# Seven copies on VectorE, one held score and a single PSUM tile in a fused attention and token-mixing kernel

## The chip, the cores and the metric

The kernel runs on one core of one Trainium2 chip. The metric is the device time of one launch in microseconds; for the kernel before it is 1265.29 us, the median of three runs (1265.22 to 1266.12).

## The reference

One input x of 2048 tokens by 512 channels goes through two branches, which a gate per token mixes:

```python
x = A_x
g = _sigmoid((x * gate_w).sum(-1, keepdims=True))
a = _A_ref(x, A_wqkv, A_wo)                   # softmax attention, H = 32 heads of Dh = 16
b = _B_ref(x, B_w1, B_b1, B_w2, B_b2)         # LayerNorm, then an MLP over the token axis (2048 -> 1792 -> 2048)
return g * a + (1 - g) * b
```

In the attention, `scores = q k^T * Dh**-0.5`, `p = softmax(scores)`, `o = p v`, and `o` is multiplied by `wo`. All of it is float32. The scores are the bulk of the elementwise work: 32 heads of 2048 by 2048, each of which has to go through an exponential.

## The kernel before

The first 278 us or so transpose x, project q, k and v, and run the first layer of the MLP. From there to about 1230 us runs the attention, with the second layer of the MLP, late query projections and output projections laid beside it. A short end (about 33 us) finishes the output.

**Groups, phases, scores.** The attention goes over 32 groups (`NG`), each two heads by half of the queries. A group has four phases (`PHASES`), so there are 128 in all. Each phase computes 16 score tiles of 128 keys by 512 queries (`NSC`), one matmul each (line 1067). A score matmul uses only one half of the rows of TensorE's array; the other half takes one "dense" matmul of the MLP or of a projection (line 1076), which runs at the same time. Most phases have 14 dense matmuls, some 12, and the last ones none.

**What happens to a score.** It lands in one of 7 PSUM banks (`BANKS`); the eighth holds the dense sum (`dn`). It takes one of three ways out. A single (`SINGLE`, six of the sixteen) is read by ScalarE, which writes exp of it to SBUF (line 1093). A pair (`TWO`, two pairs in adjacent banks) is read by one ScalarE instruction over 1024 columns (line 1031). A copied score (`EVAC`, six) is copied by VectorE from PSUM to one SBUF tile `pe` (line 1089), and at the end of the phase a single ScalarE instruction over 3072 columns takes the exponential in place (line 1102).

**Second product.** After the 16 scores TensorE multiplies exponentials by v (`apply_v`, line 963), two scores at a time, into a bank that VectorE then adds to the group's sum `ot` in SBUF (line 985). A phase applies its own singles and pairs (`TURNS`, five pairs of scores) and the copied scores of the phase before (`HELD`, three pairs of scores), since those get their exponential last. At the first phase of a group the held ones still belong to the group before, and go to a bank of their own.

**Order.** The attention is written under a manual schedule: instructions of each engine run in the order of the code, and a dependency tracker puts a semaphore wait before an instruction that touches a tile which another engine is still using. The banks are given out by hand: `shares` names which banks go to the pairs, the copies and the second product, and every score gets a PSUM tile of its own (`s0` to `s6`, then `t` for a pair, `u` for a copied score, `av`) from a pool that is opened twice in a phase (`regions`).

**Weights.** `load_weight` (line 133) brings raw blocks of the MLP's weights into `w_raw`, with four buffers; `split_weight` splits each in two parts. The first layer, before the attention, takes 64 blocks, the second layer 64 more.

Of the kernel before, what the change touches and what calls it, by code (L numbers as in the profile page):

```python
# [9 lines left out]
F32 = mybir.dt.float32  # L10
# [3 lines left out]
AF = mybir.ActivationFunctionType  # L14
# [6 lines left out]
PSUM = bass.MemoryType.PSUM  # L21
# [39 lines left out]
def gated_mix(ctx: ExitStack, tc: tile.TileContext, a_x, a_wqkv, a_wo, b_w1, b_b1, b_w2, b_b2, gate_w, out):  # L61
# [35 lines left out]
    mv = const.tile([P, NS, 2], F32, name="mv")  # L97
    rs = const.tile([P, NS], F32, name="rs")

    const.tile([P, 16], F32, name="pad")  # L100
# [34 lines left out]
    def load_weight():  # L135
        if blocks:
            src = blocks.pop(0)
            raw = wk.tile([P, NB], F32, name="w_raw", bufs=4)
            if len(src.shape) == 2:
                raw = raw[:, : src.shape[1]]  # L140
                dst = raw
            else:
                raw = raw[:, : src.shape[1] * P]
                dst = raw.rearrange("p (k s) -> p k s", s=P)
            with tc.issue_after(x_load.ins):
                nc.sync.dma_start(dst, src)
            loaded.append(raw)
# [768 lines left out]
    token, mark = (out_pool.tile([1, 1], F32, name=name, bufs=1) for name in ("token", "mark"))  # L916
# [7 lines left out]
    def shares(n):  # L924

        for one in range(0, BANKS, 2):
            lows = [k for k in range(one)][::2] + [k for k in range(one + 1, BANKS)][::2]
            for third in lows:
                if n in (third, third + 1):
                    first, second = (low for low in lows if low != third)  # L930
                    return [first, first + 1, one, second, second + 1, 2 * third + 1 - n, n]


    def regions():
        return tc.tile_pool(name="ps_s", bufs=1, space=PSUM, reuse_waits="tile")

    sums, latest, evac_done = {}, {}, []

# [49 lines left out]

    engines = {getattr(mybir.EngineType, name) for name in ("PE", "Activation", "DVE", "Pool", "SP")}
    with tc.manual_schedule(engines=engines):  # L990
        held, fence, turn, spare = [], None, 0, 0
        landed.clear()

        for p in range(LAST + 1):
# [14 lines left out]
            n_b = len(beside)  # L1009
            half = slice(0, HALF) if second else slice(HALF, P)  # L1010

            head = [second if n < n_b else (second + NSC - 1 - n) % 2 for n in range(NSC)]
            if n_b == NSC - 2:
                head[-2:] = second, 1 - second
            else:
                head[-4:] = second, 1 - second, 1 - second, second
            in_turn = list(range(n_b)) + ([14, 15] if n_b == NSC - 2 else [12, 13, 15, 14])
            qbs = {}
            for a, b in TURNS + HELD:
                if head[a] == head[b]:  # L1020
# [3 lines left out]
                    qbs[zero], qbs[one] = turn, 1 - turn  # L1024
                    turn = 1 - turn

            def exps(n):
                pt = ptp.tile([P, 2, NB], F32, name="p2", bufs=len(TWO))
                where = [share[(j - BANKS) % BANKS] for j in (n - 1, n)]
                low = min(where)  # L1030
                pairs_done.append(nc.scalar.activation(pt, twos[low, low + 1], AF.Exp, scale=SCALE))  # L1031
                for j, k in zip((n - 1, n), where):
                    units[j] = *units[j][:3], pt[:, k - low, :]

            pairs_done = []
            evac = evp.tile([P, len(EVAC), NB], F32, name="pe")
            units = {}
            share = shares(spare)
            pool = regions()
            psum = pool.__enter__()  # L1040
            ones = [psum.tile([P, NB], F32, name=f"s{n}") for n in range(BANKS)]
            for n in in_turn:
                i, qb = head[n], qbs[n]
                c = at[i][qb]
                at[i][qb] += 1
                if n < TWO[0][0]:
                    if n >= BANKS:
                        ones[share[n - BANKS]] = psum.tile([P, NB], F32, name=f"s{share[n - BANKS]}")
                    s = ones[share[n % BANKS]]
                else:  # L1050
                    if n == TWO[0][0]:
                        pool.__exit__(None, None, None)
                        pool = regions()
                        psum = pool.__enter__()
                        twos = {}
                        for low in range(BANKS):
                            if low == share[2]:
                                av = psum.tile([P, NB], F32, name="av")
                            elif low in (share[0], share[1]):
                                twos[low] = psum.tile([P, NB], F32, name=f"u{low}")  # L1060
                            elif low not in twos:
                                two = psum.tile([P, 2, NB], F32, name=f"t{low}")
                                twos[low], twos[low + 1] = two[:, 0, :], two[:, 1, :]
                                twos[low, low + 1] = two
                    s = twos[share[(n - BANKS) % BANKS]]
                rows_i = slice(i * HALF, i * HALF + ROWS)
                nc.tensor.matmul(  # L1067
                    s,
# [5 lines left out]
                if n < n_b:  # L1074
# [7 lines left out]
                if n == in_turn[-2]:  # L1082
                    if n_b and second and beside[-1][-1] in between:
                        between[beside[-1][-1]]()
                    for what, *args in amid.get(p, ()):
                        what(*args)
                if n in EVAC:
                    pt = evac[:, EVAC.index(n), :]
                    nc.vector.tensor_copy(pt, s)  # L1089
                    units[n] = i, c, qb, pt  # L1090
                elif n in SINGLE:
                    pt = ptp.tile([P, NB], F32, name="p1", bufs=len(SINGLE))
                    one = nc.scalar.activation(pt, s, AF.Exp, scale=SCALE)  # L1093
                    if n == SINGLE[-1] and p:
                        tc.add_manual_dep(one.ins, earlier.ins.name, SYNC, reason=EARLY)
                    units[n] = i, c, qb, pt
                else:
                    units[n] = i, c, qb, None
                    if n in (TWO[0][1], TWO[1][1]):
                        exps(n)  # L1100
            for x in ([evac] if p < LAST else [evac[:, :2, :], evac[:, 2:, :]]):
                done = nc.scalar.activation(x, x, AF.Exp, scale=SCALE)  # L1102
            tc.add_manual_dep(done.ins, pairs_done[0].ins.name, SYNC, reason=EARLY)
            evac_done.append(done)
            earlier = pairs_done[1]
            if n_b and second and beside[-1][-1]:
                beside[-1][-1]()
            if p == 0:
# [13 lines left out]
            spare = share[2]  # L1122
            if ph == 0:
                if held:
                    apply_v(av, grp - 1, held, final=True)
                    spare = share[3]
# [15 lines left out]
            pool.__exit__(None, None, None)  # L1142
            held = now_held
            if ph == PHASES - 1:
                assert at == [[NS, NS], [NS, NS]]


    with (
# [162 lines left out]
```

## Time and profile before

| what | value |
|---|---|
| median of three runs | 1265.29 us |
| the profiled execution's own span | 1263.6 us |
| TensorE, VectorE, ScalarE busy, of the span | 1255.3, 851.3, 1069.0 us (99, 67, 85%) |
| granted TensorE clock, mean of the span | 0.998 |
| first score of the attention | at 277.8 us |
| ScalarE busy between 400 and 1100 us | 100 us of each 100 |
| a phase in the middle of the attention (701.63 to 709.05 us) | 7.42 us |

The engines are PE (TensorE matmul), PEld (its weight load), DVE (VectorE), ACT (ScalarE), POOL and SP. Matmuls are pipelined, so PE reads as busy from the start of one to the modelled end of the next; a busy share of 99% does not say that it runs at its peak. A row of the timeline gives start, time taken, engine, line, operation and tiles, and in brackets how long the engine sat idle before it and what ended that. A row of the windows gives, after the stretch, the busy time of PE, PEld, DVE, ACT and POOL, then the granted clock, the share of the DMA engines and GB/s.

### The profile page before, as it was taken

Reading aid. Unit: us, or ns where it says so; the run is one execution under the profiler, and the core shown is the slowest. Engines: PE = TensorE matmul, PEld = TensorE weight load, DVE = VectorE, ACT = ScalarE, POOL = GpSimd, SP = SyncE. Lnnn points to the kernel's source line nnn. Section 1 sums busy time; section 2 is a strip of 40 time slices with the busy share of each in tenths; the row PEclk is TensorE's granted clock in tenths of the full one; section 3 lists DMA queues with packets and bytes.
Section 4 is the critical chain, followed back from the end, with each engine's and each line's share of the span. In section 5 each row is a group of like instructions: output and inputs, shape, how many; then the busy total and the mean of one; then the engine's idle time right before and its main releaser. Section 6 shows DMA issues by size and latency. Waiting matters only on the chain.

```text
span 1263.6 us, 32707 instructions
## 1 busy us (share of the span) xinstructions
PE 1255.3 (99%) x13342; PEld 828.5 (66%) x13342; DVE 851.3 (67%) x1562; ACT 1069.0 (85%) x1405; POOL 198.9 (16%) x316
## 2 busy tenths in 40 slices
PE   9999999999999999999999999999999999999997
PEld 7888888875666666666666666666666666666666
DVE  5675453178767676767677677776777677678883
ACT  4443343269999999999999999999999999999990
POOL 0220444461010101010101101111111111000000
PEclk9999999999999999999999999999999999999999
DMA  4799443243744444544344443443543442366611
GB/s 132 252 333 334 145 120 105 83 129 108 214 122 104 89 102 85 157 86 97 77 105 93 97 93 84 91 88 79 114 102 71 91 100 60 56 164 177 152 59 70
DMA packets 100555, 152.31 MB, mean 121 GB/s; under 512 B 17109, under 2 KB 56171, under 8 KB 96300
## 3 DMA queue, kind: packets, MB, share of 16 engines
q1 hardware_dynamic: 99820, 149.08, 45.9%
q8 instruction: 107, 1.75, 0.6%
q10 hardware_dynamic: 576, 1.05, 0.2%
q14 instruction: 52, 0.43, 0.1%
HBM read 105.39 MB, written 44.68 MB: 119 GB/s over the span
## 4 chain that ended last, share of the span: by engine, by line
PE 99%; ACT 1%; DVE 0%; issue 0%
PE av L963 31%; PE s L1067 22%; PE acc L424 12%; PE t L1067 9%; PE acc L75 8%; PE t L963 5%; PE dn L1076 4%; PE u L1067 3%; PE pa L1162 2%; PE acc L199 1%; PE acc L268 1%; PE acc L245 0%; ACT p L1093 0%; ACT pe L1102 0%; PE dn L1162 0%; PE pa L1192 0%
## 5 line engine op out<-in xcount | busy, mean ns | idle before, releaser
L1093 ACT ACTIVATE p<-s 128x512 f32<-128x512 f32 x768 | 412.4, 791 | 0.1
L1102 ACT ACTIVATE pe<-pe 128x3072 f32<-128x3072 f32 x129 | 381.7, 2961 | 0.0
L1067 PE MATMUL s<-qs,ks 64*128 64x512 f32 x1280 | 330.2, 400 | 0.6 <-ACT p L1093 0.6
L1089 DVE COPY pe<-s 128x512 f32<-128x512 f32 x512 | 318.2, 683 | 4.8 <-PE s L1067 1.1
L1067 PEld LDWEIGHTS s<-qs,ks 64*128 64x128 f32 x1280 | 225.6, 184 | 93.3 <-issue 45.3
L1031 ACT ACTIVATE p<-t 128x1024 f32<-128x1024 f32 x256 | 278.5, 1265 | 0.0
L963 PE MATMUL av<-p,v 128*32 128x256 f32 x3880 | 227.1, 379 | 0.0
L1089 DVE COPY pe<-u 128x512 f32<-128x512 f32 x256 | 164.9, 686 | 72.0 <-PE u L1067 72.0
L963 PE MATMUL av<-pe,v 128*32 128x256 f32 x3072 | 192.5, 383 | 0.0
L985 DVE TENSOR_TENSOR ot<-av,ot 128x512 f32<-128x512 f32 (+2 forms) x160 | 93.2, 583 | 142.3 <-PE av L963 141.0
L68 POOL TENSOR_TENSOR w_lo<-w_raw,w_hi 128x512 fp32r<-128x512 f32 (+1 forms) x128 | 153.1, 1203 | 197.3 <-ACT w_hi L67 100.3
L1076 PE MATMUL dn<-u_hi,w_hi 64*128 64x512 f32 x448 | 181.1, 404 | 0.0
L963 PEld LDWEIGHTS av<-p,v 128*32 128x32 f32 x3880 | 126.0, 110 | 83.3 <-ACT p L1093 0.2
L1076 PE MATMUL dn<-u_hi,w_lo 64*128 64x512 f32 x448 | 180.6, 403 | 0.0
L1076 PE MATMUL dn<-u_lo,w_hi 64*128 64x512 f32 x448 | 180.4, 403 | 0.0
L1067 PE MATMUL t<-qs,ks 64*128 64x512 f32 x512 | 142.2, 412 | 0.0
L963 PEld LDWEIGHTS av<-pe,v 128*32 128x32 f32 x3072 | 86.7, 109 | 82.1 <-ACT p L1093 37.8
L1080 POOL MEMSET token<- 1x1 f32 x128 | 11.4, 89 | 742.2 <-PE dn L1076 701.7
L67 ACT CAST w_hi<-w_raw 128x512 fp32r<-128x512 f32 (+1 forms) x67 | 38.0, 569 | 82.9 <-PE acc L424 63.1
L1067 PEld LDWEIGHTS t<-qs,ks 64*128 64x128 f32 x512 | 72.9, 184 | 51.0 <-ACT p L1093 49.5
L424 PE MATMUL acc<-h_hi,w_hi 128*128 128x512 f32 x224 | 87.9, 392 | 0.0
L424 PE MATMUL acc<-h_hi,w_lo 128*128 128x512 f32 x224 | 87.8, 392 | 0.0
(171 smaller groups left out, 1616.0 us busy)
## 6 DMA issues: line engine op xcount, KB each, us to landing
w_raw<-in_B_w_dram SPq DMA_DIRECT2D x96, 256.0 KB
ks<-kp SPq DMA_DIRECT2D x192, 128.0 KB
qs<-qp SPq DMA_DIRECT2D x256, 64.0 KB
kp<-pc SPq DMA_DIRECT2D x16, 512.0 KB
qp<-pc SPq DMA_DIRECT2D x8, 768.0 KB
qp<-row SPq DMA_DIRECT2D x24, 256.0 KB
v<-v SPq DMA_DIRECT2D x4, 1088.0 KB
x<-in_A_x_dram SPq DMA_DIRECT2D x16, 256.0 KB
```

The costliest lines, as they stand in the source:

```text
L67: copy(hi, src)
L68: return sub(lo, src, hi.bitcast(F32), ALU.subtract)
L75: nc.tensor.matmul(ps, a, b, start=start and n == 0, stop=stop and n == last)
L424: nc.tensor.matmul(p, a, b, start=first and k == 0, stop=last and k == 2)
L963: mm = nc.tensor.matmul(av[32 * j : 32 * (j + 1), i * QC : (i + 1) * QC], vb[b][:, v_at : v_at + 32], pt[:, h * QC : (h + 1) * QC], start= ...
L985: latest["add"] = nc.vector.tensor_tensor(x, y, x, ALU.add)
L1031: pairs_done.append(nc.scalar.activation(pt, twos[low, low + 1], AF.Exp, scale=SCALE))
L1067: nc.tensor.matmul(s, kt[grp][rows_i, c * P : (c + 1) * P], qt[grp][rows_i, qb * NB : (qb + 1) * NB], start=True, stop=True,)
L1076: mm = nc.tensor.matmul(ps, a[half], b[half], start=begin and not second, stop=last and bool(second))
L1089: nc.vector.tensor_copy(pt, s)
L1093: one = nc.scalar.activation(pt, s, AF.Exp, scale=SCALE)
L1102: done = nc.scalar.activation(x, x, AF.Exp, scale=SCALE)
```

## The change

The 16 scores of a phase get their way out from a string, `KINDS = "esesaaeseseeesbb"`: `e` is copied by VectorE, `s` is a single of ScalarE, `aa` and `bb` are the two pairs. So seven scores are copied, five are singles. The in-place exponential covers 3584 columns instead of 3072. The nine scores that ScalarE reads straight from PSUM are an odd number, so the last single (score 13) is held over with the seven copies: four pairs of scores are held, four are applied in their own phase. The pool of singles keeps six buffers.

The banks come from `given_out`, a small planner that walks through the 128 phases with fixed costs while the program is built, and notes for each score the bank that it takes to be free first. All seven banks are now one PSUM tile, `banks` (128 x 7 x 512), allocated once; scores, pairs and second products are slices of it. `shares`, `regions` and the per-score PSUM tiles are gone.

To make room in SBUF for the larger `pe`, `w_raw` has three buffers instead of four, `inv` one instead of two, and `token` and `mark` take the place of a pad.

```diff
-            raw = wk.tile([P, NB], F32, name="w_raw", bufs=4)
+            raw = wk.tile([P, NB], F32, name="w_raw", bufs=3)
...
-        t = out_pool.tile([P, w], F32, name="inv")[: n * DH]
+        t = out_pool.tile([P, w], F32, name="inv", bufs=1)[: n * DH]
...
-    EVAC = 1, 3, 5, 8, 14, 15
-    SINGLE = 0, 2, 4, 6, 7, 9
-    TWO = (10, 11), (12, 13)
-    TURNS = [(0, 2), (4, 6), (7, 9), *TWO]
-    HELD = [(1, 3), (5, 8), (14, 15)]
+    KINDS = "esesaaeseseeesbb"
+    SINGLES = 6
+    EVAC = [n for n, kind in enumerate(KINDS) if kind == "e"]
+    SINGLE = [n for n, kind in enumerate(KINDS) if kind == "s"]
...
+    own = sorted([(n, n) for n in SINGLE] + [(two[1], n) for two in TWO for n in two])
+    own = [n for _, n in own]
+    kept = list(EVAC)
+    if len(own) % 2:
+        own.remove(SINGLE[-1])
+        kept.append(SINGLE[-1])
+    TURNS, HELD = ([(x[i], x[i + 1]) for i in range(0, len(x), 2)] for x in (own, kept))
+    def given_out():
+
+        free, vector, scalar, stream, load, wide = [0.0] * BANKS, 0.0, 0.0, 0.0, 0.0, 0.0
+        given = []
+
+        def first_free(spread=1, at=None):
+            ways = [b for b in range(BANKS + 1 - spread)] if at is None else [at]
+            best = min(ways, key=lambda b: (max(free[b : b + spread]), b))
+            when = max(free[best : best + spread])
+            free[best : best + spread] = [1e9] * spread
+            return best, when
+
+        for p in range(LAST + 1):
...
+            for n, kind in enumerate(KINDS):
+                alone = n < singles or (n - singles) % 2 == 0
+                if kind in "es":
+                    bank[n], when = first_free()
...
+                scored[n] = start + 0.44
+                if kind == "e":
+                    vector = max(vector + 0.6, scored[n] + 0.69)
+                    free[bank[n]] = vector
+                    copied.append(vector)
+                elif kind == "s":
+                    scalar = max(scalar + 0.488, scored[n] + 0.6)
+                    free[bank[n]] = readers[n] = scalar
...
+            given.append(([bank[n] for n in range(NSC)], [b for b, _ in sums]))
+        return given
...
+        given = given_out()
+        scores_ctx = ExitStack()
+        ps_s = scores_ctx.enter_context(tc.tile_pool(name="ps_s", bufs=1, space=PSUM, reuse_waits="tile"))
+        banks = ps_s.tile([P, BANKS, NB], F32, name="banks")
...
+            bank, av_banks = given[p]
...
-                pairs_done.append(nc.scalar.activation(pt, twos[low, low + 1], AF.Exp, scale=SCALE))
+                pairs_done.append(nc.scalar.activation(pt, banks[:, low : low + 2], AF.Exp, scale=SCALE))
...
-            for n in in_turn:
+            av = banks[:, av_banks[0]]
+            for n in range(NSC):
...
-                    s = twos[share[(n - BANKS) % BANKS]]
+                s = banks[:, bank[n]]
...
-            tc.add_manual_dep(done.ins, pairs_done[0].ins.name, SYNC, reason=EARLY)
+            tc.add_manual_dep(done.ins, pairs_done[-2].ins.name, SYNC, reason=EARLY)
...
-                    av = twos[spare]
+                    av = banks[:, av_banks[1]]
```

How the built program's instructions stand, at three places. A row is the line, the operation, the tile written and the tiles read, the size, how often it is repeated, and in brackets the engines whose semaphores the instruction waits for.

TensorE at the start of a phase with dense matmuls, before. `s_...` are the tiles of single scores; `dn` is the dense sum, `qs` and `ks` the stacked queries and keys:

```order
L1067 MATMUL s_5607<-qs,ks 128x512 [waits DVE_49]
L1076 MATMUL dn<-u_hi,w_hi 128x512 [waits DVE_49,Pool_49]
L1067 MATMUL s_5608<-qs,ks 128x512
L1076 MATMUL dn<-u_lo,w_hi 128x512
L1067 MATMUL s_5606<-qs,ks 128x512 [waits PE_49]
L1076 MATMUL dn<-u_hi,w_lo 128x512
L1067 MATMUL s_5609<-qs,ks 128x512
L1076 MATMUL dn<-u_hi,w_hi 128x512
L1067 MATMUL s_5610<-qs,ks 128x512
L1076 MATMUL dn<-u_lo,w_hi 128x512
L1067 MATMUL s_5605<-qs,ks 128x512
L1076 MATMUL dn<-u_hi,w_lo 128x512
```

The same place after the change:

```order
L1097 MATMUL banks<-qs,ks 128x512 [waits DVE_49]
L1106 MATMUL dn<-u_hi,w_lo 128x512 [waits Pool_49]
L1097 MATMUL banks<-qs,ks 128x512 [waits DVE_49]
L1106 MATMUL dn<-u_hi,w_hi 128x512
L1097 MATMUL banks<-qs,ks 128x512 [waits Activation_49]
L1106 MATMUL dn<-u_lo,w_hi 128x512
L1097 MATMUL banks<-qs,ks 128x512 [waits DVE_49]
L1106 MATMUL dn<-u_hi,w_lo 128x512
L1097 MATMUL banks<-qs,ks 128x512 [waits Activation_49]
L1106 MATMUL dn<-u_hi,w_hi 128x512
L1097 MATMUL banks<-qs,ks 128x512
L1106 MATMUL dn<-u_lo,w_hi 128x512
```

Before, the scores of the first seven banks stand mostly without a wait on VectorE or ScalarE. In the changed program every score here waits for one of these two engines, and which of them it is alternates with the string `KINDS`, one place late.

TensorE from the last scores into the second product (`av`), before; `t` and `u` are the tiles of a pair and of copied scores:

```order
L1067 MATMUL t_5788<-qs,ks 128x512
L1076 MATMUL dn<-u_lo,w_hi 128x512
L1067 MATMUL u_5785<-qs,ks 128x512 [waits Activation_49]
L1067 MATMUL u_5786<-qs,ks 128x512 [waits DVE_49]
L963 MATMUL av<-pe,v_112 32x256 [waits Activation_49]
L963 MATMUL av<-pe,v_112 32x256 x11
L963 MATMUL av<-p_5743,v_112 32x256 x2
L963 MATMUL av<-p_5750,v_112 32x256 x2
L963 MATMUL av<-p_5757,v_112 32x256 x2
```

And after the change:

```order
L1106 MATMUL dn<-u_hi,w_hi 128x512
L1097 MATMUL banks<-qs,ks 128x512 [waits DVE_49]
L1106 MATMUL dn<-u_lo,w_hi 128x512
L1097 MATMUL banks<-qs,ks 128x512 [waits Activation_49]
L1097 MATMUL banks<-qs,ks 128x512
L1014 MATMUL banks<-pe,v_113 32x256 [waits Activation_49]
L1014 MATMUL banks<-pe,v_113 32x256 x13
L1014 MATMUL banks<-p_5073,v_113 32x256 x2
L1014 MATMUL banks<-p_5139,v_113 32x256 x2
```

The last two scores (pair `b`) now share one wait on ScalarE, and the second product, whose first 16 instructions are the held scores, stands behind another wait on ScalarE; it writes the same tile `banks` as the scores.

ScalarE through one phase, before:

```order
L1093 ACTIVATE p_7598<-s_7592 128x512 [waits PE_49]
L1093 ACTIVATE p_7605<-s_7591 128x512 [waits PE_49]
L1093 ACTIVATE p_7612<-s_7595 128x512 [waits PE_49]
L1093 ACTIVATE p_7619<-s_7589 128x512 [waits PE_49]
L1093 ACTIVATE p_7624<-s_7621 128x512 [waits PE_49]
L1093 ACTIVATE p_7633<-s_7630 128x512 [waits PE_49]
L1031 ACTIVATE p_7648<-t_7643 128x1024 [waits PE_49]
L1031 ACTIVATE p_7655<-t_7639 128x1024 [waits PE_49]
L1102 ACTIVATE pe<-pe 128x3072 [waits DVE_49,Activation_49]
```

And after the change:

```order
L1123 ACTIVATE p_7140<-banks 128x512 [waits PE_49]
L1123 ACTIVATE p_7147<-banks 128x512 [waits PE_49]
L1083 ACTIVATE p_7153<-banks 128x1024 [waits PE_49]
L1123 ACTIVATE p_7160<-banks 128x512 [waits PE_49]
L1123 ACTIVATE p_7167<-banks 128x512 [waits PE_49]
L1123 ACTIVATE p_7181<-banks 128x512 [waits PE_49,Activation_49]
L1083 ACTIVATE p_7185<-banks 128x1024 [waits PE_49]
L1133 ACTIVATE pe<-pe 128x3584 [waits Activation_49]
```

One instruction of 512 columns is gone, one pair has moved between the singles, and the last instruction has 512 columns more.

More of the change, by code (lines that the diff above doesn't have):

```diff
@@ L98, in gated_mix @@
     rs = const.tile([P, NS], F32, name="rs")
-    const.tile([P, 16], F32, name="pad")
+    token, mark = (const.tile([1, 1], F32, name=name) for name in ("token", "mark"))
     upper = ctx.enter_context(tc.tile_pool(name="upper", bufs=1, side="right"))
@@ L934, in regions @@
-    def regions():
-        return tc.tile_pool(name="ps_s", bufs=1, space=PSUM, reuse_waits="tile")
+    KINDS = "esesaaeseseeesbb"
+    SINGLES = 6
+    EVAC = [n for n, kind in enumerate(KINDS) if kind == "e"]
+    SINGLE = [n for n, kind in enumerate(KINDS) if kind == "s"]
+    TWO = [tuple(n for n, kind in enumerate(KINDS) if kind == two) for two in sorted(set(KINDS) - {"e", "s"})]
+    assert all(len(two) == 2 for two in TWO) and len(KINDS) == NSC
+    own = sorted([(n, n) for n in SINGLE] + [(two[1], n) for two in TWO for n in two])
@@ L1010, in gated_mix @@
             half = slice(0, HALF) if second else slice(HALF, P)
[L1012 to L1017, printed above, removed]
+            head = [second if n < n_b else (second + n - n_b) % 2 for n in range(NSC)]
             qbs = {}
@@ L1025, in gated_mix, with exps @@
                     turn = 1 - turn
-            def exps(n):
+            bank, av_banks = given[p]
+            def exps(two):
                 pt = ptp.tile([P, 2, NB], F32, name="p2", bufs=len(TWO))
[L1029 to L1033, printed above, removed]
+                low = bank[two[0]]
+                assert bank[two[1]] == low + 1
+                pairs_done.append(nc.scalar.activation(pt, banks[:, low : low + 2], AF.Exp, scale=SCALE))
+                for k, j in enumerate(two):
+                    units[j] = *units[j][:3], pt[:, k, :]
             pairs_done = []
@@ L1037, in gated_mix @@
             units = {}
[L1038 to L1041, printed above, removed]
-            for n in in_turn:
+            av = banks[:, av_banks[0]]
+            for n in range(NSC):
                 i, qb = head[n], qbs[n]
@@ L1045, in gated_mix @@
                 at[i][qb] += 1
[L1046 to L1064, printed above, removed]
-                    s = twos[share[(n - BANKS) % BANKS]]
+                s = banks[:, bank[n]]
                 rows_i = slice(i * HALF, i * HALF + ROWS)
```

56 lines of the change are left out of this document (39 added, 17 removed).

## The prediction

> **What bounds the kernel now.** I read the windows over a phase first, then the timeline of each engine in that phase, then the list of waits. Two phases in the middle of the attention (busy time of PE, PEld, DVE, ACT, POOL; then the granted clock), and below them the timeline of ScalarE, TensorE and VectorE at the end of the first of the two:
>
> ```profile
> 701.63:709.05 7.42, 7.42 (x98) 4.56 (x95) 4.75 (x10) 7.42 (x10) 1.92 (x3) 1.00 0.47 83
> 709.05:716.47 7.42, 7.42 (x98) 4.54 (x94) 4.40 (x8) 7.42 (x10) 0.25 (x2) 1.00 0.63 80
> ...
> 702.16 3.24 ACT L1093 ACTIVATE p<-s 128x512 f32<-128x512 f32 x6
> 705.05 2.19 ACT L1031 ACTIVATE p<-t 128x1024 f32<-128x1024 f32 x2
> 706.88 3.01 ACT L1102 ACTIVATE pe<-pe 128x3072 f32<-128x3072 f32 x1
> 709.58 0.80 ACT L1093 ACTIVATE p<-s 128x512 f32<-128x512 f32 x1
> ...
> 705.06 0.41 PE L1067 MATMUL u<-qs,ks 64*128 64x512 f32 x2
> 705.46 1.50 PE L963 MATMUL av<-pe,v 128*32 128x256 f32 x24
> 706.78 2.34 PE L963 MATMUL av<-p,v 128*32 128x256 f32 x40
> 709.05 0.50 PE L1067 MATMUL s<-qs,ks 64*128 64x512 f32 x1
> ...
> 709.19 0.69 DVE L985 TENSOR_TENSOR ot<-av,ot 128x512 f32<-128x512 f32 x1 [1.85 <-PE av L963]
> ```
>
> A phase takes 7.42 us. ScalarE fills it without a pause: six singles in 2.89 us (702.16 to 705.05, 0.48 each), two pairs in 1.83 (0.915 each), the in-place exponential in 2.70 (706.88 to 709.58). TensorE is nearly as tight: 16 scores from 701.63 to 705.46, the second product from there to 709.05. This works because seven banks let 16 scores run ahead of their readers: matmul, copy and exponential of different scores overlap. VectorE has 2.7 us to spare.
>
> **The change: what ScalarE gains.** One 512-column single goes (0.48 us), 512 columns are added to the in-place exponential. A pair costs 0.915 and a single 0.48, so 512 more columns cost 0.43. ScalarE needs 7.36 us instead of 7.42; over 128 phases that is 7 us. VectorE gets one copy more, which fits in its spare time. That is all the split itself can bring.
>
> **The change: what the single tile does.** This decides. In the rows of the changed program a score waits for VectorE or ScalarE at nearly every place: VectorE, VectorE, ScalarE, VectorE, ScalarE, none, against the kinds e, s, e, s, a, a. Score 0 waits for VectorE; that is its last read of `banks`, the add of the phase before. So when score 1 waits for VectorE again, it can only be for something that VectorE does later, and the first such thing is the copy of score 0. In the same way the second product has waited for ScalarE's pair `b`, ScalarE's last read of PSUM; the wait of score 2 for ScalarE can only be for the exponential of score 1. The tracker takes the seven slices for one object: each score waits until the score before it has been read. The pair's second score has no wait, since nothing is read between the two. The second product waits for the exponential of pair `b`, the add for the second product, the next phase's score 0 for the add. PSUM no longer lets anything run ahead, and a phase is one chain: matmul, reader, matmul, reader.
>
> What one step of that chain costs is seen wherever the old kernel ran into such a wait. Rows of the timeline near the start of the attention, the start of a later phase, and the durations (least, median, greatest, ns) of three lines:
>
> ```profile
> 285.87 0.66 ACT L1093 ACTIVATE p<-s 128x512 f32<-128x512 f32 x1
> 286.58 0.18 PEld L1067 LDWEIGHTS s<-qs,ks 64*128 64x128 f32 x1 [1.00 <-ACT p L1093]
> 286.58 0.50 PE L1067 MATMUL s<-qs,ks 64*128 64x512 f32 x1 [0.57 <-ACT p L1093]
> ...
> 286.92 0.39 PE L1067 MATMUL s<-qs,ks 64*128 64x512 f32 x1
> 287.35 0.69 DVE L1089 COPY pe<-s 128x512 f32<-128x512 f32 x1 [0.57 <-PE dn L1076]
> ...
> 278.57 0.39 PE L1067 MATMUL s<-qs,ks 64*128 64x512 f32 x1
> 279.00 0.60 ACT L1093 ACTIVATE p<-s 128x512 f32<-128x512 f32 x1
> ...
> 716.47 0.49 PE L1067 MATMUL s<-qs,ks 64*128 64x512 f32 x1
> 716.81 0.39 PE L1067 MATMUL s<-qs,ks 64*128 64x512 f32 x1
> ...
> L1093 ACT ACTIVATE p<-s x768: 578/802/872, 278.3 to 1224.2; 128x512 f32<-128x512 f32 x192
> L1031 ACT ACTIVATE p<-t x256: 1068/1281/1325, 281.4 to 1225.6; 128x1024 f32<-128x1024 f32 x128
> L1089 DVE COPY pe<-s x512: 678/681/694, 278.8 to 1223.8; 128x512 f32<-128x512 f32 x171
> ```
>
> An exponential ended at 286.53 and the waiting score started at 286.58: 0.05. That score took 0.50, not 0.39, because its weights were loaded only then. From its end to the reader it is 0.04 (287.31 to 287.35; 278.96 to 279.00). A copy takes 0.68. An exponential takes 0.60 on an idle ScalarE; the median of 0.80 has the one before it still in the pipe. For a pair I take the least, 1.07, as here too ScalarE is idle.
>
> - seven copied scores: 0.05 + 0.50 + 0.04 + 0.68 = 1.27 each, 8.89 us
> - five singles: 0.05 + 0.50 + 0.04 + 0.60 = 1.19 each, 5.95
> - pair a: the second score starts 0.34 after the first and ends 0.73 after it; 0.05 + 0.73 + 0.04 + 1.07 = 1.89
> - pair b: its scores are in different halves of the array, side by side: 0.05 + 0.50 + 0.04 + 1.07 = 1.66
> - second product: 0.05 and the 3.66 from 705.46 to 709.12, 3.71
> - the add: 0.07 (709.12 to 709.19) + 0.69, 0.76
>
> Together 22.86 us, three times the old phase. The in-place exponential (3.0 + 0.43) lies beside the second product, the add and the next score 0, 5.7 us, and costs nothing; without that cover ScalarE would be late at the first single. VectorE's casts and other work (4.75 less six copies and the add, some 0.5) lies beside pair b and the second product.
>
> The rest: 31 group starts have their second product in two parts, with the first part's adds between (0.42 and as much again below, with two handovers and the restart of the product, by the rows above about 1.2): 37 us. Before the attention and after its last second product:
>
> ```profile
> 277.77 0.50 PE L1067 MATMUL s<-qs,ks 64*128 64x512 f32 x1
> 701.83 0.42 DVE L985 TENSOR_TENSOR ot<-t,ot 128x256 f32<-128x256 f32 x1 [1.04 <-issue]
> 1228.44 0.61 PE L963 MATMUL av<-pe,v 128*32 128x256 f32 x8
> 160.00:277.00 117.00, 117.00 (x510) 95.20 (x508) 48.10 (x61) 48.74 (x87) 58.62 (x51) 1.00 0.35 104
>   DMA w_raw<-in_B_w_dram: 0.9, 1
> ```
>
> 277.8 us before it and 35 after (1228.4 to 1263.6) stay. Three raw weight blocks instead of four: 64 blocks feed a stage in which TensorE has no gap (117.00 of 117.00 us), and its loads caused one wait of 0.9 us in the run. I take 0; were every block to wait that long, 58 us. In the attention the loads get three times as long. `inv` with one buffer is used eight times, phases apart: 0. At full clock the span is 277.8 + 128 x 22.86 + 37 + 35 = 3276.
>
> **The clock.** The last question is whether TensorE keeps its clock when it works a fifth of the time. The ends of the run show both directions:
>
> ```profile
> 1.21 2.74 PE L245 MATMUL acc<-idle 128*128 128x512 bf16 x6 [1.21 <-DVE idle L240]
> 5.48 0.79 PE L268 MATMUL acc<-wv_hi,xt_hi 128*128 128x512 f32 x1
> 6.07 0.63 PE L268 MATMUL acc<-wv_lo,xt_hi 128*128 128x512 f32 x1
> 9.33 0.62 PE L268 MATMUL acc<-wv_hi,xt_lo 128*128 128x512 f32 x2
> ...
> 1252.54:1255.95 3.41, 3.41 (x16) 2.74 (x16) 0.75 (x1) 0.00 (x0) 0.00 (x0) 1.00 0.22 82
> 1255.95:1259.36 3.41, 1.24 (x6) 0.67 (x4) 0.75 (x1) 0.00 (x0) 0.00 (x0) 1.00 0.38 140
> 1259.36:1263.60 4.24, 0.00 (x0) 0.00 (x0) 0.00 (x0) 0.00 (x0) 0.00 (x0) 0.50 0.09 29
> ```
>
> At the end the clock fell to 0.50 after a stretch of 3.41 us in which TensorE was busy for 1.24, or 36%. In the changed scores it is busy 0.50 of 1.2 us, 40% with the weight load in it, and streams 0.23 of 1.27, 18%. So I expect the clock to fall among the scores. At the start matmuls were slow (0.43 apart, 0.63 long) and became fast (0.23 apart, 0.39 long) after about 5 us of nearly unbroken work; so in the second product the clock should come back after some 5 us.
>
> Priced: a lone score takes 0.63 to 0.79 instead of 0.39 to 0.50, so 0.27 more; 14 of them and 0.20 for the second score of pair a, 3.98. The second product, 3.45 of matmuls, runs 5 us at half rate (2.5 done) and 0.95 at full: 2.5 more. What then stays fast for another one or two such stretches is worth up to four scores, 1.1 to 1.2 back. 22.86 + 3.98 + 2.5 - 1.2 = 28.1. The span: 277.8 + 128 x 28.1 + 37 + 35 = 3947. The profiled span of before is 1263.6 against a median of 1265.3; the same 1.7 on top gives **3950 us**.
>
> **Rivals.**
>
> *The clock stays full:* 3276 + 1.7, 3278 us. For it: the fall at 1259.36 came after 2.2 us of no matmul at all (the last ended at about 1257.2), while between serial scores TensorE never rests over 1.2 us. Against it: the share of work.
>
> [...]
>
> *The waits are met early, and the scores still overlap:* then ScalarE sets a phase at 7.36 us and the kernel comes out 7 us faster, 1258. It would need each wait to be for an older reader of the same bank, seven scores back, done before TensorE asks; it turns as soon as the wait is for the score just before. The alternation of the two engines speaks against it, and nothing else for it but the seven banks.
>
> *The clock stays at half throughout:* the second product then costs 3.45 more, nothing comes back: 22.86 + 3.98 + 3.45 = 30.3, 4230 us.
>
> **How the numbers follow.** The clock falls and comes back in each phase, 0.54; it stays full, 0.34; always half, 0.06; the scores overlap, 0.06. Less than 0.2% either way is what a measurement of this kernel can't tell from no change. The first three cases are far slower, 0.94 together; the last would be faster by 0.6% (0.05), or have its 7 us eaten by late banks and show no change (0.01). The bounds of the unknown costs: an exponential at 0.58 or 0.80 moves the phase by -0.1 to +1.0, a lone slow score at 0.63 or 0.79 by 0.5 each way. The range takes in the full clock below and the first case with its bounds above: 3200 to 4080.
>
> **What would show it.** In the changed profile ScalarE should be far from full, about 7 of 28 us; TensorE should wait before each score for the reader of the score before, near 1.2 us, VectorE's copy behind seven and ScalarE behind seven; the median of line 1123 should drop from 802 ns to about 600, that of 1083 from 1281 to 1070. The granted clock in the middle should be between 0.5 and 0.8. It is wrong if 16 scores still take under 5 us, if the attention's clock reads 1.00 (then 3278), or if a phase is far from 28 at such a clock.

## The result, and the profile after

The changed kernel takes 3987.4 us (median of four runs, 3982.6 to 3988.9) against 1265.4 us: 3.151 times the time of before, 95% interval 3.146 to 3.155. The prediction was 3950 us.

The page of the changed kernel, its busy times, the granted clock in 40 slices and the chain that ended last:

```profile
PE 2401.7 (60%) x13342; PEld 1073.2 (27%) x13342; DVE 998.3 (25%) x1698; ACT 1157.2 (29%) x1277; POOL 196.0 (5%) x316
PEclk9996565656656566665656656565656555565657
PE 62%; DVE 18%; ACT 16%; issue 3%; DMA 0%; DVEq 0%; SPq 0%; POOL 0%; ACTq 0%
```

No engine is full any more. The chain now runs through TensorE, VectorE and ScalarE in turn, and in the slices of the attention the clock is at five or six tenths, seven in the last. What TensorE's weight loads and matmuls waited for (total us, times, the longest):

```profile
PEld banks L1097 <- DVE pe L1119: 1031.8, 833, 1.3
PEld banks L1097 <- ACT p L1123: 743.0, 640, 1.5
...
PE banks L1097 <- DVE pe L1119: 649.7, 833, 0.8
```

640 waits for the singles are five in each of 128 phases, so every single is waited for; the 833 for the copies are out of 896. In before's list the largest wait of a score's load was 49.5 us in all. One phase in the timeline, from its first score to the next phase's (weight loads, dense matmuls, most readers and what only repeats are left out):

```profile
706.08 0.49 PE L1097 MATMUL banks<-qs,ks 64*128 64x512 f32 x1 [0.89 <-DVE ot L1036]
706.61 0.69 DVE L1119 COPY pe<-banks 128x512 f32<-128x512 f32 x1 [0.58 <-PE dn L1106]
...
707.35 0.50 PE L1097 MATMUL banks<-qs,ks 64*128 64x512 f32 x1 [0.77 <-DVE pe L1119]
707.89 0.60 ACT L1123 ACTIVATE p<-banks 128x512 f32<-128x512 f32 x1 [6.15 <-PE dn L1106]
...
708.54 0.79 PE L1097 MATMUL banks<-qs,ks 64*128 64x512 f32 x1 [0.68 <-ACT p L1123]
...
710.12 0.79 PE L1097 MATMUL banks<-qs,ks 64*128 64x512 f32 x1 [0.78 <-DVE pe L1119]
...
711.59 0.79 PE L1097 MATMUL banks<-qs,ks 64*128 64x512 f32 x1 [0.68 <-ACT p L1123]
...
713.93 0.79 PE L1097 MATMUL banks<-qs,ks 64*128 64x512 f32 x1 [1.11 <-ACT p L1083]
...
726.29 0.79 PE L1097 MATMUL banks<-qs,ks 64*128 64x512 f32 x2 [0.75 <-ACT p L1123]
...
728.21 2.79 PE L1014 MATMUL banks<-pe,v 128*32 128x256 f32 x24 [1.12 <-ACT p L1083]
...
733.75 0.69 DVE L1036 TENSOR_TENSOR ot<-banks,ot 128x512 f32<-128x512 f32 x1 [6.47 <-PE banks L1014]
...
734.49 0.50 PE L1097 MATMUL banks<-qs,ks 64*128 64x512 f32 x1 [0.89 <-DVE ot L1036]
```

Matmul, reader, matmul, reader: no score starts before the one ahead of it is read. At full clock a copied score costs 1.27 us (706.08 to 707.35) and a single 1.19 (707.35 to 708.54); at half clock, from 708.54 on, a copy costs 1.58 and a single 1.47. The phase is 28.41 us; over all of them the mean from first score to first score is 28.66, since the first phase of a group takes 1.0 more than the others (29.4).

The clock at the windows in which it changes (after the stretch: busy time of PE, PEld, DVE, ACT, POOL; granted clock; the last two columns are DMA):

```profile
329.00:332.41 3.41, 3.41 (x36) 1.58 (x32) 0.00 (x0) 2.76 (x2) 0.00 (x0) 0.50 0.04 9
332.41:335.82 3.41, 2.01 (x30) 0.79 (x22) 1.16 (x2) 0.00 (x0) 0.00 (x0) 1.00 0.00 0
335.82:339.24 3.42, 1.50 (x6) 0.56 (x6) 0.92 (x2) 0.74 (x2) 0.00 (x0) 1.00 0.00 0
339.24:342.65 3.41, 1.79 (x6) 0.79 (x6) 0.00 (x0) 1.48 (x2) 0.00 (x0) 0.50 0.00 0
```

In this trace's records of the clock every stretch of the attention is a whole number of steps of 3.413 us: full for one step (39 times) or two (86 times), then half, but for a few places, for six or seven. Above, the step filled by the second product (3.41 of 3.41 busy) is followed by a full one, and the step with six score matmuls (1.50 of 3.42 busy) by a half one: TensorE was at work in the step before the fall at 339.24, and between the first fall and the last rise of this trace it rests for at most 1.2 us at a time.

### The profile page after: what moved, and what is told of

Read it like the earlier page. It is cut to its first block, busy times and chain, and to the rows that moved or that the text cites. A ratio compares the mean times of both kernels' runs of the same rounds, so it can differ in the third digit from the quotient of the medians.

```text
span 3980.8 us, 32376 instructions
## 1 busy us (share of the span) xinstructions
PE 2401.7 (60%) x13342; PEld 1073.2 (27%) x13342; DVE 998.3 (25%) x1698; ACT 1157.2 (29%) x1277; POOL 196.0 (5%) x316
## 4 chain that ended last, share of the span: by engine, by line
PE 62%; DVE 18%; ACT 16%; issue 3%; DMA 0%; DVEq 0%; SPq 0%; POOL 0%; ACTq 0%
PE banks L1097 35%; PE banks L1014 18%; DVE pe L1119 15%; ACT p L1123 10%; ACT p L1083 7%; PE acc L424 4%; DVE ot L1036 3%; PE acc L75 3%; PE dn L1106 2%; PE pa L1191 1%; DMA r<-ot 0%; PE acc L199 0%; PE acc L268 0%; DVEq L1036 0%; DMA wv_raw<-in_A_wqkv_dram 0%
## 5 line engine op out<-in xcount | busy, mean ns | idle before, releaser
L1097 PE MATMUL banks<-qs,ks 64*128 64x512 f32 x2048 | 1370.0, 731 | 1404.5 <-DVE pe L1119 649.7
L1097 PEld LDWEIGHTS banks<-qs,ks 64*128 64x128 f32 x2048 | 501.0, 270 | 2271.8 <-DVE pe L1119 1031.8
L1123 ACT ACTIVATE p<-banks 128x512 f32<-128x512 f32 x640 | 382.4, 598 | 2344.1 <-PE dn L1106 1738.3
L1119 DVE COPY pe<-banks 128x512 f32<-128x512 f32 x896 | 619.7, 692 | 1743.7 <-PE dn L1106 1613.1
L1014 PE MATMUL banks<-pe,v 128*32 128x256 f32 x3584 | 448.5, 623 | 142.3 <-ACT p L1083 142.3
L1014 PE MATMUL banks<-p,v 128*32 128x256 f32 x4608 | 394.3, 449 | 25.3 <-DVE ot L1036 24.1
L1133 ACT ACTIVATE pe<-pe 128x3584 f32<-128x3584 f32 x129 | 407.4, 3159 | 0.0
L1083 ACT ACTIVATE p<-banks 128x1024 f32<-128x1024 f32 x256 | 262.2, 1024 | 281.6 <-PE banks L1097 146.9
L1014 PEld LDWEIGHTS banks<-pe,v 128*32 128x32 f32 x3584 | 173.0, 166 | 375.2 <-ACT p L1083 206.5
L1014 PEld LDWEIGHTS banks<-p,v 128*32 128x32 f32 x4608 | 191.8, 136 | 194.8 <-issue 84.2
```

Source lines behind the costliest of these rows:

```text
L1014: mm = nc.tensor.matmul(av[32 * j : 32 * (j + 1), i * QC : (i + 1) * QC], vb[b][:, v_at : v_at + 32], pt[:, h * QC : (h + 1) * QC], start= ...
L1083: pairs_done.append(nc.scalar.activation(pt, banks[:, low : low + 2], AF.Exp, scale=SCALE))
L1097: nc.tensor.matmul(s, kt[grp][rows_i, c * P : (c + 1) * P], qt[grp][rows_i, qb * NB : (qb + 1) * NB], start=True, stop=True,)
```

## The experiments

### Only the single tile, and everything but it

The first kernel is before, with its six copies, order and weight buffers, and one PSUM tile for the seven banks (its main lines):

```diff
-            ones = [psum.tile([P, NB], F32, name=f"s{n}") for n in range(BANKS)]
+        banks = ps_s.tile([P, BANKS, NB], F32, name="banks")
...
-                        ones[share[n - BANKS]] = psum.tile([P, NB], F32, name=f"s{share[n - BANKS]}")
-                    s = ones[share[n % BANKS]]
+                    s = banks[:, share[n % BANKS]]
```

> The kernel before with one thing changed: its seven banks are slices of one PSUM tile. Six copies, six singles, the old order, four raw weight blocks stay. Theory (the single tile alone serialises the phase): 6 x 1.27 + 6 x 1.19 + 2 x 1.89 + 3.71 + 0.76 = 23.0 us a phase at full clock, and with the clock that the changed kernel was granted (0.60) close to its time: 3950 to 4050 us. Rival (the seven copies, the order or the planner's banks make the chain): 1265 us, no change.

It took 3982 us in its one run, within 0.2% of the changed kernel. The two waits of its weight loads in the list of waits:

```profile
PEld banks L1052 <- ACT p L1078: 870.0, 768, 1.2
PEld banks L1052 <- DVE pe L1074: 789.5, 640, 1.3
```

And a window in the middle of it, where the clock reads 0.61 as in the changed kernel:

```profile
1000.00:2000.00 1000.00, 579.84 (x3276) 229.80 (x3276) 196.83 (x344) 293.73 (x315) 28.84 (x63) 0.61 0.11 26
```

768 waits are all six singles of every phase. The tile alone is enough for the chain and the fall of the clock; copies, order and planner are not needed for it.

The second kernel is the changed one, with the planner's banks, but a tile for each score, pair and sum:

```diff
-        banks = ps_s.tile([P, BANKS, NB], F32, name="banks")
...
-                s = banks[:, bank[n]]
+                if KINDS[n] in "es":
+                    s = tile_of(n)
+                else:
+                    s = tile_of(KINDS[n])[:, KINDS[: n].count(KINDS[n]), :]
```

`tile_of` opens a pool of seven banks, laid out as the planner's plan has them, whenever the plan uses a bank a second time.

> The changed kernel with everything kept (seven copies, the new order of kinds, the planner's banks, three raw weight blocks), except that each score, each pair and each second product gets a PSUM tile of its own, so that the tracker sees seven things and not one. Theory (the single tile is the whole loss, the order and the split are as good as the old ones): 1258 us, 7 below before. Rival (the planner's plan of banks and the new order also cost, since pair b needs two neighbouring banks late in the phase; my walk of the banks with the durations of before gives up to 7.87 us a phase against 7.42): 1275 to 1322 us. Rival (the order or the split are what makes the phase serial): near 3987 us.

1328.7 us, 1.0498 times before (1.0481 to 1.0516): the chain is gone, but 63 us of loss remain that the single tile had covered up. So the rival on the rest of the change holds, with 7 us more than its upper bound, and the 7 us of gain that the prediction gave the split are not there. The next three kernels take the 63 us apart.

### Three raw weight blocks

```diff
-            raw = wk.tile([P, NB], F32, name="w_raw", bufs=4)
+            raw = wk.tile([P, NB], F32, name="w_raw", bufs=3)
```

The one buffer for `inv`, as in the changed kernel, goes with it.

> The kernel before with only the small edits of buffers: three raw weight blocks, not four, and one buffer for the inverse of the sums. Theory (loads are issued far enough ahead): 1265 us, within 0.2% of before. Rival (each of the 64 blocks before the attention waits for its load, 0.9 us as the one wait that the trace of before shows): up to 58 us more, 1323.

1277.3 us, 1.0095 times before (1.0078 to 1.0112): 12 us, and not before the attention, whose first score is at 277.75 us as in before. One phase, at 869 us, takes 8.2 us longer than its counterpart; two others lose 1.6 and 1.7. SyncE's queue ahead of it, and then VectorE's and TensorE's rows (all of this kernel):

```profile
850.19 0.38 SPq L146 DMA_DIRECT2D w_raw<-in_B_w_dram  x1
...
861.21 0.38 SPq L146 DMA_DIRECT2D w_raw<-in_B_w_dram  x1
861.65 0.50 SPq L949 DMA_DIRECT2D o<-ot  x1
...
865.94 4.05 SPq L470 DMA_DIRECT2D ks<-kp  x6
870.03 0.42 SPq L695 DMA_DIRECT2D row<-in_A_wo_dram  x1
...
875.45 0.43 DVE L67 CAST big<-row 128x512 fp32r<-128x512 f32 x1 [8.56 <-DMA row<-in_A_wo_dram]
...
877.26 0.79 PE L1067 MATMUL s<-qs,ks 64*128 64x512 f32 x1 [6.45 <-DVE ot L985]
```

The second weight load had no free buffer and held SyncE's queue from 850.57 to 861.21. Behind it stood eight stores, six loads of `ks` and a row of `wo`; VectorE came to that row's split before the row had landed, and behind the split stood the add for which TensorE's next score waits. In before both loads went out at once and the row was issued at 856.41:

```profile
845.80 0.94 SPq L146 DMA_DIRECT2D w_raw<-in_B_w_dram  x2
...
856.41 0.42 SPq L695 DMA_DIRECT2D row<-in_A_wo_dram  x1
```

To test that reading, the same kernel with the rows of `wo` loaded one phase earlier:

```diff
-                    call(2 * at + 5 + 4 * k, load_wo, k, 2 * at + 5 + 4 * k)
+                    call(2 * at + 4 + 4 * k, load_wo, k, 2 * at + 5 + 4 * k)
```

> Three raw weight blocks as in three_raw, but each row of the last weight (wo) is loaded one phase earlier; VectorE's split of it stays where it was. In three_raw SyncE held a weight block's load for 11 us until a buffer was free, the row behind it was loaded 13.6 us later than before, and VectorE waited 8.56 us for it. Theory (that one wait is most of the 12 us): 1277.3 - 8.2 = 1269 us. Rival (the loss is made again elsewhere, since the queue stays late and what stands behind the rows now waits in their place): 1277 us.

1268.75 us, 1.0028 times before (1.0018 to 1.0038): 8.6 us come back where 8.2 were expected, and the clock no longer falls on the way, as it does for 6.8 us behind that wait in three_raw. So of the 12 us some two thirds are this one row. The remaining 3.3 lie mostly where three_raw lost its 1.6 and 1.7: in this trace the same two phases take 1.9 and 1.5 us longer than in before. Why was not followed, and neither was the part of `inv`.

### The split alone

Before's own tiles, banks and kind of order, with seven copies, and the three raw blocks that they need for room:

```diff
-    EVAC = 1, 3, 5, 8, 14, 15
-    SINGLE = 0, 2, 4, 6, 7, 9
+    EVAC = 1, 3, 5, 7, 9, 14, 15
+    SINGLE = 0, 2, 4, 6, 8
...
-    TURNS = [(0, 2), (4, 6), (7, 9), *TWO]
-    HELD = [(1, 3), (5, 8), (14, 15)]
+    TURNS = [(0, 2), (4, 6), *TWO]
+    HELD = [(1, 3), (5, 7), (8, 9), (14, 15)]
```

> The kernel before with its own tiles, its own rule for the banks and its old kind of order, but seven copies and five singles (copies 1, 3, 5, 7, 9, 14, 15; a single held over with the seventh copy) and the three raw weight blocks that this needs for room. Without the split, three raw blocks gave 1277.3. Theory (the split is worth what the prediction said, ScalarE 0.06 us a phase shorter, VectorE's copy in spare time): 1270 us. Rival (VectorE binds: the add and seven copies at 0.60 each end about 5.5 us after the phase's first score, the in-place exponential of seven then ends 0.4 us later than that of six, ScalarE frees the next phase's banks later; my walk of the phase gives 7.71 against 7.43 us): 1277 + 128 x 0.28 = 1313 us, and the new order with the planner costs the other 16 us of own_tiles.

1299.3 us, 1.0265 times before (1.0247 to 1.0282), so 22.0 us above three raw blocks alone. The sign is the rival's, the size some 60% of its 36 us. The median phase is 7.58 us instead of 7.42, which makes 20.5 of the 22. ScalarE's and VectorE's rows over two phases of it (the second begins at 707.50):

```profile
703.28 1.97 ACT L1030 ACTIVATE p<-t 128x1024 f32<-128x1024 f32 x2
...
704.26 1.27 DVE L1088 COPY pe<-u 128x512 f32<-128x512 f32 x2
...
705.63 3.20 ACT L1101 ACTIVATE pe<-pe 128x3584 f32<-128x3584 f32 x1 [0.38 <-DVE pe L1088]
...
707.50 0.49 PE L1066 MATMUL s<-qs,ks 64*128 64x512 f32 x1
...
708.73 2.53 ACT L1092 ACTIVATE p<-s 128x512 f32<-128x512 f32 x5
...
711.12 1.98 ACT L1030 ACTIVATE p<-t 128x1024 f32<-128x1024 f32 x2
711.40 0.41 PE L1066 MATMUL u<-qs,ks 64*128 64x512 f32 x2
...
711.83 1.29 DVE L1088 COPY pe<-u 128x512 f32<-128x512 f32 x2 [0.49 <-PE u L1066]
...
713.21 3.20 ACT L1101 ACTIVATE pe<-pe 128x3584 f32<-128x3584 f32 x1
```

The five singles take 2.39 us (708.73 to 711.12) and the longer in-place exponential 3.10 until the next single (705.63 to 708.73), as the prediction had it. But from the first pair to the in-place exponential it is 2.35 and 2.09 us, where before needs 1.83 (705.05 to 706.88): the exponential of seven starts 0.1 after VectorE's last copy and can't go ahead. 2.39 + 2.09 + 3.10 = 7.58. And by these rows the last copies are late because ScalarE is: its first single starts 1.23 us into the phase shown (0.53 in before), so banks come free later and the last two scores run at 3.90 us instead of 3.43. The phase shown is a late one; the medians over the attention are 0.98 and 3.64.

VectorE has time to spare over a phase, but not between the last score and the in-place exponential, and that was so ahead of the change. VectorE's last two copies in before, in the phase of the prediction's rows:

```profile
705.50 1.29 DVE L1089 COPY pe<-u 128x512 f32<-128x512 f32 x2 [0.62 <-PE u L1067]
```

They end at 706.79, and the in-place exponential starts 0.09 later, at 706.88; over the attention the median of this distance is 0.10 in both kernels.

If the parts simply add up, which was not tested, own_tiles' 63 us are 12 for the raw blocks, 22 for the split and some 29 that are left to the new order of kinds, the planner's banks and the pools that own_tiles opens for them. Which of these takes the 29 was not separated.

### Keeping the clock up

These four are the changed kernel with matmuls of the same operands added behind the scores, into two tiles that nobody reads (the planner has five banks then). The first has one, in the half of the array's rows that the score uses:

```diff
+        unread = [ps_s.tile([P, NB], F32, name=f"unread{i}") for i in range(2)]
...
+                for _ in range(1 if n not in (4, 14, 15) else 0):
+                    nc.tensor.matmul(
+                        unread[i],
...
```

> As with three added matmuls a score, but with one: TensorE streams 0.46 of a step of 1.2 us, 0.37 of the time among the scores. Before's last stretch showed the clock fall behind 3.41 us of which TensorE was busy in 1.24, a share of 0.36. Theory (the share of busy time decides, and 0.36 is too little): clock near 0.60 as without it, 3950 to 4000 us. Rival (any second matmul a step is enough): clock 1.00 and about 3276 us.

The second has three, in the same half:

```diff
+                for _ in range(3 if n not in (4, 14, 15) else 0):
```

> The changed kernel with five banks and two unread tiles: behind 13 of the 16 scores of a phase come three more matmuls of the same operands whose results nobody reads (16 scores become 55 matmuls). Nothing waits for them and they fit into the time that TensorE waits: 4 x 0.23 = 0.92 us of a step of 1.2. Theory (the clock falls because TensorE is busy for too little of the time, and the chain itself is 22.9 us at full clock): clock 1.00, 128 x 22.86 + 350 = 3276 us, 700 us less with three times the score matmuls. Rival (the clock falls for another reason, for example the many waits): clock near 0.60, four matmuls then take 4 x 0.46 = 1.84 us, longer than the step at half clock, and the time rises to 4200 or more.

In the third they alternate between the halves, so that two run side by side:

```diff
+                for f in (1 - i, i, 1 - i) if n not in (4, 14, 15) else ():
```

> As with three added matmuls a score (which ran at a clock of 0.94 and 3454 us), but the added ones alternate between the two halves of the array's rows, the first in the half that the score does not use. The number of matmuls is the same, 55 a phase for 16 scores, but they run two side by side: two slots of 0.23 us, 0.46 of a step of 1.2 us, as long as with one added matmul (clock 0.64 and 3972 us). Theory A (the clock follows the share of the time in which TensorE is busy): as with one added matmul, clock 0.60 to 0.65, 3950 to 4000 us. Theory B (it follows how much of the array works, time by rows): as with three, clock 0.93 or more, 3350 to 3470 us.

And in the fourth there are five, behind the last score too:

```diff
+                for f in (1 - i, i, 1 - i, i, 1 - i) if n not in (4, 14) else ():
```

> Five added matmuls behind 14 of the 16 scores, the last score too, alternating between the halves of the rows: three slots of 0.23 us in each step of 1.2, with both halves in use, and now also beside the wait for pair b, behind which the run with three added matmuls fell back to half (PEclk 0.94). Theory B (the work of the array decides): clock 1.00 throughout, 128 x 22.86 + 350 = 3276 us; with the queue of added matmuls at half clock (3 x 0.46 = 1.4 us) as long as a step. Theory A (the share of busy time, 0.69 of 1.2, less than with three in one half): clock below 0.94, 3500 to 3900 us.

Each of the four has one run:

| kernel | matmuls added behind a score | time, us | mean clock of the run |
|---|---|---|---|
| changed | none | 3987 | 0.630 |
| fill_one | 1, same half | 3972 | 0.636 |
| fill_three | 3, same half | 3454 | 0.936 |
| fill_sides | 3, alternating | 3448 | 0.936 |
| fill_all | 5, alternating, the last score too | 3286 | 0.999 |

With five added, TensorE issues 8960 matmuls more whose results go nowhere, and the kernel is 701 us faster. Its median phase is 22.96 us, where the prediction's sum at full clock was 22.86, and its time 3286 where 3276 was expected. So the fallen clock costs the changed kernel some 700 us, and the chain itself some 2000.

Three added did not quite suffice (0.936, not 1.00): in its trace the clock still fell 79 times, the last at its end, and mostly within a microsecond or so of the start of a second product, ahead of which pair b is waited for and that kernel adds none. Covering that place as well, with five instead of three, brings 1.00.

fill_one and fill_sides bear on two readings of the clock. Their windows in the middle, first fill_one:

```profile
1000.00:2000.00 1000.00, 743.13 (x3732) 313.22 (x3730) 224.05 (x383) 283.84 (x280) 28.53 (x63) 0.61 0.12 27
```

and fill_sides:

```profile
1000.00:2000.00 1000.00, 738.24 (x5450) 364.02 (x5452) 267.57 (x460) 333.48 (x330) 32.18 (x72) 0.95 0.14 30
```

TensorE reads as busy for the same 74% in both, yet one runs at 0.61 and the other at 0.95. fill_three has as many matmuls as fill_sides, is busy 86% of the time, and has the same clock. These means alone don't settle it: at half clock the same matmul reads as busy for longer (0.79 us instead of 0.50 above), so fill_one's 74% comes in part from its low clock. Single steps at full clock are cleaner, one each of fill_one, fill_sides and fill_three:

```profile
1022.08:1025.49 3.41, 2.19 (x9) 0.88 (x9) 0.69 (x1) 0.98 (x2) 0.00 (x0) 1.00 0.86 98
...
1021.25:1024.66 3.41, 2.23 (x15) 1.17 (x14) 0.69 (x1) 1.24 (x2) 0.00 (x0) 1.00 0.00 0
...
861.57:864.98 3.41, 3.08 (x11) 1.51 (x10) 2.79 (x6) 0.68 (x2) 0.62 (x2) 1.00 0.13 49
```

Behind the first and the third the clock fell to half; behind the second it stayed full. The first two are equally busy with 9 and 15 matmuls, and the third is the busiest, with 11. Busy time alone doesn't part these three, then; the work in a step (matmuls, or rows of the array in use) goes with it better, though no count of it parts all the steps of these traces. Three steps in the windows of fill_three say the same of the way up:

```profile
308.61:312.02 3.41, 3.18 (x10) 2.42 (x10) 0.87 (x2) 0.60 (x1) 0.00 (x0) 0.50 0.00 0
...
335.92:339.33 3.41, 3.41 (x37) 1.58 (x32) 0.00 (x0) 1.19 (x2) 0.00 (x0) 0.50 0.00 0
339.33:342.74 3.41, 2.43 (x22) 1.26 (x13) 1.38 (x2) 0.00 (x0) 0.00 (x0) 1.00 0.00 0
```

Ten matmuls of scores and added ones, each on half the rows, fill 3.18 of 3.41 us and the clock stays at half; behind 37 matmuls, mostly of the second product, which uses all rows (128*32 in the timeline, a score 64*128), it is full in the next step. Whether the measure is the number of matmuls or the part of the array they use was not separated.

No version here beats the kernel before. The nearest, three raw blocks with the early row, is 3 us slower, and the split for which the fourth block was given up costs time by itself in the one order in which it was tried.

## Why the prediction was right, and where its terms were off

**The single tile makes the phase a chain: right.** The tile alone gives 3982 us, and the waits are of the predicted kind, each score for the reader of the score before. ScalarE works 8.1 of 28.4 us (about 7 predicted). The median of line 1123 went to 597 ns (600 predicted), that of line 1083 to 1024 (1070).

**The steps at full clock: right.** A copied score 1.27 and a single 1.19 us in the timeline, as priced; the phase at full clock 22.96 against 22.86. The in-place exponential stays hidden beside the second product.

**The clock falls and comes back in each phase: right, with sizes that were off and partly cancel.** Over the 95 phases within a group, the scores cost 21.97 us on average up to the second product, 3.58 more than the 18.39 at full clock; the prediction had 3.98 less 1.2, so 2.78. A slow score costs 0.31 more behind a copy and 0.28 behind a single in the phase shown, where 0.27 was priced. The 1.2 given back was too much: two scores of the phase shown stay fast, none to four in others and 2.4 on average, not always four. The second product with the handover to the add takes 5.70 us on average (5.54 in the phase shown, 728.21 to 733.75) against the 6.2 priced (3.71 + 2.5), since the clock is back sooner than after 5 us: in the phase shown after 3.56, at 731.77. Together 28.4 for a phase within a group against 28.1; 0.3 over 128 phases is about what 3950 was low by (37). That it is no more is in part luck, as the scores were 0.8 too low and the second product 0.5 too high. The group starts were priced at 37 us and take 31 (1.0 each).

The reason given for the fall, a busy share of some 40%, did not hold: fill_three's clock fell behind a step that was 90% busy (3.08 of 3.41 us). The forecast of a fall came out all the same, because the lone scores are little by either measure: six matmuls, 1.50 us busy, in the step before the fall at 339.24.

**The rival of the full clock** would have given 3278 us; with enough matmuls to hold the clock, 3286 was measured. Its sum was right and its condition was not met. **The rival of the overlap** fails twice: the waits aren't met early, and where the tiles let the scores overlap the kernel comes out at 1328.7 us, not 1258.

**The split's gain: wrong, in sign.** The step that failed is "VectorE gets one copy more, which fits in its spare time". Of the spare 2.7 us of a phase 1.85 lie after the last copy, and 0.62 are a wait for the last scores. By itself, in before's order, the split costs 22 us instead of gaining 7. The sum for 3950 did not use this gain.

**The raw blocks at 0: wrong by 12 us at before's pace.** The prediction looked for waits before the attention, bounded them at 58 us, and took none. For the attention it leaned on the longer phases, and did not ask what stands behind the load on SyncE's queue where the phases stay short. In the changed kernel next to nothing of the split and the blocks shows: with six copies and four blocks, only_tile took 3982 us against 3987. That is why the total was near in spite of them; that the long phases are what covers them was not tested.

## What to carry to other kernels

Banks that engines are to use at the same time must be separate objects to whatever sets the waits; a plan of banks is worth nothing if the tracker sees one tile (only_tile: 1265 us to 3982). When a change makes TensorE wait between small matmuls, price the clock as well as the waits (some 700 of the changed kernel's 3987 us). An engine's spare time is only worth something at the place where the chain passes (VectorE had 2.7 us of a phase to spare, and the split alone cost 22 us), and a load that waits for a buffer delays everything behind it on its queue (SyncE's by 10.6 us in three_raw, 850.57 to 861.21).

## What the hardware showed beyond that

The clock was expected to follow how long TensorE is busy. In the steps compared it went with the work instead: at full clock a step of fill_one with 2.19 us busy and 9 matmuls was followed by half clock, one of fill_sides with 2.23 us and 15 by full clock. In the changed kernel's trace the change came in steps of 3.413 us, up as well as down, so that most of its phases, 28 us long, hold one or two fast steps. Unread matmuls, 8960 of them, took 18% off a kernel's time (3987 to 3286 us). The clock of the changed kernel swung between half and full with rests of TensorE of at most 1.2 us in its phases.
